# Linear attention on one core: the first head loaded whole, the last head's q work in halves, a longer warm-up matmul, and new per-engine orders

## Chip, core and metric

One core of a Trainium2 chip runs the whole program. The time is the device time of one execution in microseconds (us); lower is better. Eight executions of the kernel before are at hand, median 173.31 us, from 172.78 to 173.74.

## What is computed

Inputs q, k and v and the output have the shape (1, 32, 2048, 128) in bf16. For each of the 32 heads:

```python
phi(x) = where(x > 0, x + 1, exp(x)) + 1e-6
kv  = phi(k)^T @ v          # 128 x 128
z   = sum over s of phi(k)  # 128
out = (phi(q) @ kv) / (phi(q) . z + 1e-6)
```

## The kernel before, in words

A head's q, k and v are 2048 rows of 128. Partition p of the 128 holds rows 16p to 16p+15, so a whole head is one tile of 128 x (16 x 128), 4 KB a partition and 512 KB in all; half a head, 8 of the 16 rows, is 2 KB a partition. `phi` is split in two summands, min(exp(x), 1) + eps and max(x, 0), and each is multiplied by TensorE on its own, so they are never added up outside PSUM.

The steps of head h carry short keys, and these keys are what the orders are made of:

- `ldq`, `ldk`, `ldv` (L300, SP queue): the loads, into a ring of NI = 7 heads. `st` (L392, SP queue): the store, from a ring of NO = 12 heads. A load waits until the ring place is free, a store until its products are done. All go through one queue, in order.
- `ek` (L312, ACT): exp of k. `em` (L315, DVE): min with 1, plus eps. `rkd` (L318, DVE) and `rkp` (L322, POOL): max(k, 0) of rows 0 to 7 and of rows 8 to 15. `v1` (L326, POOL): a copy of v beside a column of ones.
- `kv` (L333, PE): 32 matmuls in two halves of 16 into one PSUM group. `kvs` (L338, ACT): its copy to SBUF.
- `T` (L344, PE): 16 transposes of q into PSUM. `eq` (L347, ACT): exp of it. `emq` (L349, DVE): min and eps. `rqa` (L353, ACT) and `rqb` (L356, DVE): max(q, 0) of rows 0 to 7 and 8 to 15. There is one transposed tile, so `T` of a head waits for `eq`, `rqa` and `rqb` of the head before.
- `n` (L363, L368, L370, PE): phi(q) times kv for 12 rows (`n.0`, four banks) and 4 rows (`n.1`, two banks), after a small matmul that sets eps. `r` (L377, DVE): reciprocal of the denominators. `f` (L384, DVE): the products, which also free the banks. The last head has three such groups of 6, 6 and 4 rows.
- `w` (L291, PE): matmuls of the identity into an unused bank, 120 columns each, in three groups of 60, 15 and 15 (`WARM`, L12). They compute nothing that is used; w2, and so the first of them in the order, waits for the identity.

What decides which rows a step covers are the functions `k_parts`, `q_parts`, `v_parts` (L17 to L21): two halves for head 0, whole for all others. In the kernel before, loads and steps share these.

The order of the work is written out by hand for each of the five engines (`ORDER`, L60 to L120) as a list of keys. `Program.resolve` (L158) works out the semaphore waits from the dependencies that `head` (L303) states; an engine executes its list strictly in order, so what stands behind a waiting step waits too. From head 3 on `gate` (L54) holds back the two POOL steps: `v1` of head h until `r.0` of head h - 3 is done, `rkp` until `f.0` of head h - 3 is done.

```python
def k_parts(h):
    return HALVES if h == 0 else WHOLE

q_parts = v_parts = k_parts
```

Of the kernel before, what the change touches and what calls it, by code (L numbers as in the profile page):

```python
# [21 lines left out]

# [31 lines left out]
def gate(name, h):  # L54
    if h < 3:
# [5 lines left out]
    "PE": """  # L61
        w2 T0.1 T0.0 w1 w0 T1.0 kv0.0 kv0.1 n0.0 kv1.0 kv1.1 T2.0 n0.1 n1.0 kv2.0 kv2.1 T3.0 n1.1 kv3.0 kv3.1 n2.0
        T4.0 n2.1 kv4.0 kv4.1 n3.0 T5.0 n3.1 kv5.0 kv5.1 n4.0 T6.0 n4.1 kv6.0 kv6.1 n5.0 T7.0 n5.1 kv7.0 kv7.1 n6.0
# [12 lines left out]
        f2.0 em5.0 rqb4 r2.1 rkd6.0 f2.1 r3.0 emq4.0 f3.0 em6.0 rqb5 r3.1 rkd7.0 f3.1 r4.0 emq5.0 f4.0 em7.0 rqb6
        r4.1 f4.1 r5.0 emq6.0 f5.0 em8.0 rqb7 r5.1 f5.1 rkd8.0 r6.0 emq7.0 f6.0 em9.0 rqb8 r6.1 f6.1 rkd10.0 rkd9.0
        r7.0 emq8.0 f7.0 rkd11.0 rqb9 r7.1 em10.0 f7.1 r8.0 emq9.0 f8.0 em11.0 rqb10 r8.1 f8.1 rkd12.0 r9.0 emq10.0
        f9.0 em12.0 r9.1 rqb11 f9.1 emq11.0 r10.0 rkd13.0 f10.0 em13.0 rqb12 r10.1 f10.1 rkd14.0 r11.0 emq12.0 f11.0
# [12 lines left out]
        eq0.1 eq0.0 rqa0 ek0.0 ek1.0 ek0.1 eq1.0 kvs0 rqa1 ek2.0 kvs1 ek3.0 eq2.0 rqa2 kvs2 ek4.0 eq3.0 kvs3 rqa3
        ek5.0 eq4.0 kvs4 rqa4 ek6.0 eq5.0 kvs5 rqa5 ek7.0 eq6.0 kvs6 rqa6 ek8.0 eq7.0 kvs7 rqa7 ek9.0 eq8.0 kvs8
# [14 lines left out]
    "SP": """  # L108
        ldq0.0 ldq0.1 ldk0.0 ldk0.1 ldk1.0 ldq1.0 ldv0.0 ldv0.1 ldv1.0 ldk2.0 ldq2.0 ldk3.0 ldv2.0 ldq3.0 ldk4.0
        ldv3.0 ldv4.0 ldq4.0 ldk5.0 ldv5.0 ldv6.0 ldq5.0 ldk6.0 ldk7.0 ldv7.0 ldk8.0 ldq6.0 ldk9.0 ldv8.0 ldq7.0  # L110
        ldq8.0 st0.0 ldk10.0 ldq9.0 st1.0 ldv9.0 ldv10.0 ldv11.0 ldq10.0 ldk11.0 ldk12.0 ldk13.0 ldv12.0 ldv13.0
        ldq11.0 st2.0 ldq12.0 st3.0 ldq13.0 ldq14.0 ldk14.0 ldv14.0 ldk15.0 ldv15.0 st4.0 ldk16.0 ldq15.0 ldk17.0
        ldq16.0 ldv16.0 ldv17.0 ldv18.0 ldk18.0 ldq17.0 ldk19.0 ldq18.0 st5.0 ldv19.0 ldk20.0 ldk21.0 ldq19.0
        ldq20.0 ldv20.0 ldv21.0 ldv22.0 ldv23.0 ldk22.0 st6.0 st7.0 st8.0 ldk23.0 ldq21.0 ldk24.0 ldq22.0 ldk25.0
        ldv24.0 ldk26.0 ldq23.0 ldq24.0 ldk27.0 st9.0 ldv25.0 st10.0 ldq25.0 ldv26.0 st11.0 ldq26.0 ldv27.0 st12.0
        ldk28.0 ldk29.0 ldq27.0 st13.0 ldv28.0 st14.0 ldk30.0 ldq28.0 ldv29.0 ldq29.0 ldq30.0 st15.0 ldv30.0 ldv31.0
        ldk31.0 ldq31.0 st16.0 st17.0 st18.0 st19.0 st20.0 st21.0 st22.0 st23.0 st24.0 st25.0 st26.0 st27.0 st28.0
        st29.0 st30.0 st31.0 st31.1 st31.2
    """,
# [97 lines left out]
def bass_standalone__linear_attn_elu__prompt_kernel(nc: bass.Bass, q: bass.AP, k: bass.AP, v: bass.AP, out: bass.AP):  # L217
# [11 lines left out]
    with ExitStack() as es:  # L229
# [73 lines left out]
        def head(h):  # L303
            for i, (a, b) in enumerate(k_parts(h)):
                load("k", k_sb, kf, h, i, a, b, freed(NI, h, ("ek", k_parts), ("rkd", rkd_parts), ("rkp", rkp_parts)))
            for i, (a, b) in enumerate(q_parts(h)):
                load("q", q_sb, qf, h, i, a, b, freed(NI, h, ("T", q_parts)))
            for i, (a, b) in enumerate(v_parts(h)):
                load("v", v_sb, vf, h, i, a, b, freed(NI, h, ("v1", v_parts)))

# [30 lines left out]
            for i, (a, b) in enumerate(q_parts(h)):  # L341
                def g(e, a=a, b=b):
                    for j in range(a, b):
                        ins = e.transpose(xT[:, j], q_sb[:, h % NI, j], ident[:])  # L344
# [2 lines left out]
                add("ACT", f"eq{h}.{i}", lambda e, a=a, b=b: e.activation(emq_sb[:, h % NQ, a:b], xT[:, a:b], ACT.Exp),  # L347
# [109 lines left out]
```

## Time and profile before

| what | value |
|---|---|
| median of 8 executions | 173.31 us (172.78 to 173.74) |
| profiled execution, its time | 173.48 us |
| its span, first to last instruction | 171.6 us |
| busy share: PE, PE weight load, DVE, ACT, POOL | 94%, 93%, 91%, 89%, 50% |
| granted TensorE clock, mean | 0.982 |
| data moved | 67.52 MB, 394 GB/s over the span |
| `eq` whole head, `ek` whole head (mean) | 1877 ns, 1912 ns, x31 each |
| `f` of 12 rows, `f` of 4 rows (mean) | 1744 ns, 682 ns |
| store at the end (128 KB), issue to landing | 1.8 us |

Durations are of one profiled execution. A row "18.21 0.28 ACT L338 ... [0.93 <-PE la L333]" means: at 18.21 us from the span's start ACT began line 338, which took 0.28 us, after 0.93 us without work which a step of PE's line 333 ended. Neighbouring durations overlap a little[...]; the distance between starts is what a step costs in a row of steps. Issues on the SP queue are not work: what counts for them is the landing, which is the time of the last of 16 completion events of a DMA.

### The profile page before, as it was taken

How to read it: one execution, taken by the hardware profiler on the slowest of the kernel's cores; microseconds unless marked ns; L12 is line 12 of the kernel's file. 1: busy time of each engine (PE TensorE's matmuls, PEld its weight loads, DVE VectorE, ACT ScalarE, POOL GpSimd, SP SyncE). 2: the span in 40 equal slices, each digit the busy share in tenths (PEclk: the TensorE clock that was granted, in tenths of full speed). 3: DMA queues.
4: the chain of work that ended last, by engine and by line, in shares of the span. 5: the costliest groups of instructions: out<-in, count | busy, mean ns of one | idle time of the engine just before them, and what ended most of it. 6: DMA issues, size and time to landing. Idle time of an engine off the chain costs nothing.

```text
span 171.6 us, 6462 instructions
## 1 busy us (share of the span) xinstructions
PE 161.3 (94%) x2842; PEld 158.9 (93%) x2842; DVE 156.2 (91%) x266; ACT 153.4 (89%) x131; POOL 85.2 (50%) x71
## 2 busy tenths in 40 slices
PE   3898989999999999999999999999999999999771
PEld 3898889999999999999999999999999999999770
DVE  0539999999999999999999999999999999999883
ACT  2699789999999999999999999999999999996600
POOL 1255545566644664556655566555555555463000
PEclk9999999999999999999999999999999999999975
DMA  4999999999999999999999999999999999999874
GB/s 163 359 421 407 408 408 410 408 404 420 410 415 407 412 417 410 416 410 406 416 412 411 411 415 416 407 411 416 415 415 419 413 425 410 416 415 415 324 305 146
DMA packets 19179, 67.52 MB, mean 394 GB/s; under 512 B 2128, under 2 KB 2512, under 8 KB 19152
## 3 DMA queue, kind: packets, MB, share of 16 engines
q1 hardware_dynamic: 19152, 67.12, 97.5%
q8 instruction: 22, 0.36, 0.8%
q14 instruction: 5, 0.04, 0.1%
HBM read 50.33 MB, written 16.78 MB: 391 GB/s over the span
## 4 chain that ended last, share of the span: by engine, by line
ACT 56%; PE 28%; DVE 11%; DMA 2%; issue 2%; SPq 0%; DVEq 0%
ACT la L347 22%; ACT la L312 21%; ACT la L353 10%; PE la L333 10%; PE la L368 6%; PE la L370 6%; PE la L344 5%; DVE la L384 5%; ACT la L338 3%; DMA la<-in_q_dram 2%; DVE la L318 2%; DVE la L349 2%; DVE la L315 1%; DVE la L356 1%; PE la L363 1%
## 5 line engine op out<-in xcount | busy, mean ns | idle before, releaser
L384 DVE TENSOR_TENSOR la<-la 128x1536 bf16<-128x1536 f32 (+2 forms) x65 | 77.7, 1197 | 0.7
L370 PE MATMUL la<-la 128*128 128x129 bf16 x512 | 69.1, 222 | 0.0
L368 PE MATMUL la<-la 128*128 128x129 bf16 x512 | 69.0, 220 | 0.0
L347 ACT ACTIVATE la<-la 128x2048 bf16<-128x2048 bf16 (+1 forms) x33 | 60.1, 1825 | 6.1 <-PE la L344 3.9
L333 PE MATMUL la<-la 128*128 128x129 bf16 x1024 | 64.0, 219 | 0.5 <-DVE la L315 0.5
L326 POOL COPY la<-la 128x1024 int32<-128x1024 int32 (+1 forms) x33 | 40.6, 1233 | 41.5 <-DVE la L377 34.2
L312 ACT ACTIVATE la<-la 128x2048 bf16<-128x2048 bf16 (+1 forms) x33 | 61.2, 1861 | 0.0
L333 PEld LDWEIGHTS la<-la 128*128 128x128 bf16 x1024 | 60.0, 97 | 0.7 <-DVE la L315 0.7
L322 POOL TENSOR_SCALAR la<-la 128x1024 bf16<-128x1024 bf16 x32 | 44.0, 1374 | 29.4 <-DVE la L384 23.8
L370 PEld LDWEIGHTS la<-la 128*128 128x128 bf16 x512 | 49.9, 97 | 0.0
L368 PEld LDWEIGHTS la<-la 128*128 128x128 bf16 x512 | 47.6, 98 | 0.0
L344 PE MATMUL la<-la 128*128 128x128 bf16 x512 | 34.6, 222 | 1.6 <-DMA la<-in_q_dram 1.6
L363 PE MATMUL la<-la 128*128 128x3 bf16 (+1 forms) x192 | 32.5, 169 | 2.9 <-DVE la L384 2.3
L353 ACT ACTIVATE la<-la 128x1024 bf16<-128x1024 bf16 x32 | 32.6, 1018 | 0.0
L344 PEld LDWEIGHTS la<-la 128*128 128x128 bf16 x512 | 30.0, 99 | 2.0 <-DMA la<-in_q_dram 1.8
L315 DVE TENSOR_SCALAR la<-la 128x2048 bf16<-128x2048 bf16 (+1 forms) x33 | 22.8, 695 | 2.9 <-ACT la L312 2.8
L349 DVE TENSOR_SCALAR la<-la 128x2048 bf16<-128x2048 bf16 (+1 forms) x33 | 22.6, 684 | 1.4 <-ACT la L347 1.3
L363 PEld LDWEIGHTS la<-la 128*128 128x128 bf16 x192 | 18.9, 98 | 4.4 <-DVE la L384 3.2
L356 DVE TENSOR_SCALAR la<-la 128x1024 bf16<-128x1024 bf16 x32 | 21.8, 680 | 1.2 <-ACT la L347 0.5
L318 DVE TENSOR_SCALAR la<-la 128x1024 bf16<-128x1024 bf16 x32 | 15.0, 475 | 5.5 <-DMA la<-in_k_dram 5.4
L377 DVE RECIPROCAL la<-la 128x12 f32<-128x12 f32 (+2 forms) x65 | 12.8, 198 | 1.1 <-PE la L370 0.4
L338 ACT ACTIVATE la<-la 128x129 bf16<-128x129 f32 x32 | 9.0, 282 | 1.5 <-PE la L333 1.5
(14 smaller groups left out, 15.9 us busy)
## 6 DMA issues: line engine op xcount, KB each, us to landing
la<-in_k_dram SPq DMA_DIRECT2D x31, 512.0 KB, 15.5
la<-in_q_dram SPq DMA_DIRECT2D x31, 512.0 KB, 15.5
la<-in_v_dram SPq DMA_DIRECT2D x31, 512.0 KB, 15.2
out_dram<-la SPq DMA_DIRECT2D x31, 512.0 KB, 15.2
la<-in_q_dram SPq DMA_DIRECT2D x2, 256.0 KB, 3.1
la<-in_k_dram SPq DMA_DIRECT2D x2, 256.0 KB, 4.1
la<-in_v_dram SPq DMA_DIRECT2D x2, 256.0 KB, 6.3
out_dram<-la SPq DMA_DIRECT2D x2, 192.0 KB, 2.1
```

The costliest lines, as they stand in the source:

```text
L312: add("ACT", f"ek{h}.{i}", lambda e, a=a, b=b: e.activation(em_sb[:, h % NE, a:b], k_sb[:, h % NI, a:b], ACT.Exp), [f"ldk{h}.{i}"] + freed ...
L322: add("POOL", f"rkp{h}.{i}", lambda e, a=a, b=b: e.tensor_scalar(rk_sb[:, h % NR, a:b], k_sb[:, h % NI, a:b], BIG, 0.0, op0=ALU.min, op1=A ...
L326: add("POOL", f"v1{h}.{i}", lambda e, a=a, b=b: e.tensor_copy(v1_sb[:, h % NV, a:b, 0:D].bitcast(i32), v_sb[:, h % NI, a:b].bitcast(i32)), ...
L333: ins = e.matmul(kv_ps, lhsT=src[:, j], rhs=v1_sb[:, h % NV, j, 0:NC], start=(j + part == 0), stop=(j == NT - 1 and part == 1))
L344: ins = e.transpose(xT[:, j], q_sb[:, h % NI, j], ident[:])
L347: add("ACT", f"eq{h}.{i}", lambda e, a=a, b=b: e.activation(emq_sb[:, h % NQ, a:b], xT[:, a:b], ACT.Exp), [f"T{h}.{i}"] + freed(NQ, h, ("n ...
L349: add("DVE", f"emq{h}.{i}", lambda e, a=a, b=b: e.tensor_scalar(emq_sb[:, h % NQ, a:b], emq_sb[:, h % NQ, a:b], 1.0, EPS, op0=ALU.min, op1 ...
L353: add("ACT", f"rqa{h}", lambda e: e.activation(rq_sb[:, h % NQ, 0:n], xT[:, 0:n], ACT.Relu), over("T", h, q_parts, 0, n) + freed(NQ, h, (" ...
L363: e.matmul(_ap(o_ps[:, :], o + D, [[NC, m]]), lhsT=ones[:], rhs=epsr[:, 0:m], start=True, stop=False, skip_group_check=True)
L368: e.matmul(to, lhsT=emq_sb[:, h % NQ, t], rhs=kvs_sb[:, h % NK], start=False, stop=False, skip_group_check=True)
L370: ins = e.matmul(to, lhsT=rq_sb[:, h % NQ, t], rhs=kvs_sb[:, h % NK], start=False, stop=True, skip_group_check=True)
L384: return e.tensor_tensor(out=_ap(o_sb[:, :, :, :], first(o_sb[:, h % NO, t0, 0:1]) - first(o_sb[:, :, :, :]), [[m * D, nb], [D, m], [1, D] ...
```

## The change

The loads of head 0 are whole, while its other steps stay in halves: a new `ld_parts` returns whole for every head, and each step that reads a load now waits for all loads that overlap its rows. `q_parts` gives halves for head 31 also, so that `T31`, `eq31` and `emq31` become two steps each. The warm-up matmul has 480 columns (the 120 columns of the identity read four times) and the groups are 15, 4 and 4. All five orders are new.

```diff
-WARM = (60, 15, 15)
+WARM = (15, 4, 4)
...
-q_parts = v_parts = k_parts
+def ld_parts(h):
+    return WHOLE
+
+
+v_parts = k_parts
+
+
+def q_parts(h):
+    return HALVES if h in (0, NH - 1) else WHOLE
...
     "PE": """
-        w2 T0.1 T0.0 w1 w0 T1.0 kv0.0 kv0.1 n0.0 kv1.0 kv1.1 T2.0 n0.1 n1.0 kv2.0 kv2.1 T3.0 n1.1 kv3.0 kv3.1 n2.0
+        w2 w1 T0.0 T0.1 w0 kv0.0 kv0.1 T1.0 n0.0 kv1.0 kv1.1 T2.0 n0.1 n1.0 kv2.0 kv2.1 T3.0 n1.1 kv3.0 kv3.1 n2.0
...
-        kv28.1 n27.0 T29.0 n27.1 kv29.0 kv29.1 n28.0 T30.0 n28.1 kv30.0 kv30.1 n29.0 T31.0 n29.1 kv31.0 kv31.1 n30.0
-        n30.1 n31.0 n31.1 n31.2
+        kv28.1 n27.0 T29.0 n27.1 kv29.0 kv29.1 n28.0 T30.0 n28.1 kv30.0 kv30.1 n29.0 T31.0 n29.1 T31.1 kv31.0 kv31.1
+        n30.0 n30.1 n31.0 n31.1 n31.2
...
     "DVE": """
-        rkd0.0 ones v1ones0 emq0.1 rqb0 emq0.0 rkd1.0 em0.0 em0.1 v1ones1 eps0 eps1 em1.0 eps2 emq1.0 rqb1 r0.0 f0.0
-        rkd3.0 rkd2.0 em2.0 em3.0 rqb2 emq2.0 r0.1 f0.1 r1.0 rkd4.0 f1.0 em4.0 rqb3 r1.1 rkd5.0 f1.1 r2.0 emq3.0
+        rkd0.0 v1ones0 v1ones1 eps0 ones em0.0 eps1 rkd1.0 em0.1 rqb0 eps2 emq0.0 emq0.1 em1.0 r0.0 f0.0 rqb1 rkd2.0
+        emq1.0 rkd3.0 em2.0 r1.0 em3.0 rqb2 emq2.0 r0.1 f0.1 f1.0 rkd4.0 em4.0 rkd5.0 r1.1 rqb3 f1.1 r2.0 emq3.0
...
-        rqb29 r27.1 emq29.0 f27.1 r28.0 em30.0 f28.0 em31.0 rqb30 r28.1 f28.1 r29.0 rkd31.0 f29.0 emq30.0 emq31.0
-        rqb31 r29.1 r30.0 f29.1 f30.0 r30.1 f30.1 r31.0 f31.0 r31.1 f31.1 r31.2 f31.2
+        rqb29 r27.1 rkd30.0 f27.1 r28.0 emq29.0 f28.0 em31.0 rqb30 r28.1 f28.1 r29.0 rkd31.0 f29.0 emq30.0 rqb31
+        r29.1 emq31.0 f29.1 r30.0 f30.0 r30.1 emq31.1 f30.1 r31.0 f31.0 r31.1 f31.1 r31.2 f31.2
...
     "ACT": """
-        eq0.1 eq0.0 rqa0 ek0.0 ek1.0 ek0.1 eq1.0 kvs0 rqa1 ek2.0 kvs1 ek3.0 eq2.0 rqa2 kvs2 ek4.0 eq3.0 kvs3 rqa3
+        rqa0 eq0.1 ek0.0 ek0.1 eq0.0 ek1.0 kvs0 eq1.0 rqa1 ek2.0 kvs1 ek3.0 eq2.0 rqa2 kvs2 ek4.0 eq3.0 kvs3 rqa3
...
-        ek30.0 eq29.0 kvs29 rqa29 ek31.0 eq30.0 kvs30 rqa30 eq31.0 rqa31 kvs31
+        ek30.0 eq29.0 kvs29 rqa29 ek31.0 eq30.0 kvs30 rqa30 eq31.1 eq31.0 kvs31 rqa31
...
     "SP": """
-        ldq0.0 ldq0.1 ldk0.0 ldk0.1 ldk1.0 ldq1.0 ldv0.0 ldv0.1 ldv1.0 ldk2.0 ldq2.0 ldk3.0 ldv2.0 ldq3.0 ldk4.0
+        ldq0.0 ldk0.0 ldv0.0 ldk1.0 ldq1.0 ldv1.0 ldk2.0 ldq2.0 ldk3.0 ldv2.0 ldk4.0 ldq3.0 ldv3.0 ldk5.0 ldq4.0
...
-                ins = e.matmul(o_ps[:, 512 + 3 * NC:512 + 3 * NC + 120], lhsT=ident[:], rhs=ident[:, 0:120],
+                ins = e.matmul(o_ps[:, 512:992], lhsT=ident[:], rhs=_ap(ident[:, :], 0, [[0, 4], [1, 120]]),
...
-            for i, (a, b) in enumerate(q_parts(h)):
+            for i, (a, b) in enumerate(ld_parts(h)):
                 load("q", q_sb, qf, h, i, a, b, freed(NI, h, ("T", q_parts)))
...
-                    [f"ldk{h}.{i}"] + freed(NE, h, ("kv", kv_parts)))
+                    over("ldk", h, ld_parts, a, b) + freed(NE, h, ("kv", kv_parts)))
```

On POOL one pair is exchanged (`v13.0` now ahead of `rkp3.0`). In the SP list the loads of the last heads stand later: `ldv31` is the 113th transfer in units of 512 KB instead of the 110th, `ldq31` the 116th instead of the 112th. In the middle DVE's list is made of the same steps per head, in a few rotations of `emq`, `r`, `rkd` and `rqb`.

More of the change, by code (lines that the diff above doesn't have):

```diff
@@ L75 @@
-        rkd3.0 rkd2.0 em2.0 em3.0 rqb2 emq2.0 r0.1 f0.1 r1.0 rkd4.0 f1.0 em4.0 rqb3 r1.1 rkd5.0 f1.1 r2.0 emq3.0
[L76 to L79, printed above, removed]
@@ L80 @@
-        em14.0 r11.1 rqb13 f11.1 rkd15.0 r12.0 emq13.0 f12.0 em15.0 r12.1 rqb14 f12.1 rkd16.0 r13.0 emq14.0 f13.0
-        em16.0 r13.1 rqb15 f13.1 rkd17.0 r14.0 emq15.0 f14.0 em17.0 r14.1 rqb16 f14.1 rkd18.0 r15.0 emq16.0 f15.0
-        em18.0 rqb17 r15.1 rkd19.0 f15.1 r16.0 emq17.0 f16.0 em19.0 rqb18 r16.1 rkd20.0 f16.1 r17.0 emq18.0 f17.0
-        em20.0 rqb19 r17.1 rkd21.0 f17.1 r18.0 emq19.0 f18.0 em21.0 rqb20 r18.1 f18.1 rkd22.0 r19.0 emq20.0 f19.0
-        em22.0 rqb21 r19.1 f19.1 rkd23.0 r20.0 emq21.0 f20.0 em23.0 rqb22 r20.1 rkd24.0 f20.1 r21.0 emq22.0 f21.0
@@ L85 @@
-        em24.0 r21.1 rqb23 f21.1 emq23.0 r22.0 rkd25.0 f22.0 em25.0 rqb24 r22.1 f22.1 rkd26.0 emq24.0 r23.0 f23.0
-        em26.0 r23.1 rqb25 f23.1 emq25.0 r24.0 rkd27.0 f24.0 em27.0 rqb26 r24.1 f24.1 emq26.0 r25.0 f25.0 em28.0
-        rqb27 r25.1 f25.1 rkd29.0 r26.0 rkd28.0 f26.0 emq27.0 rqb28 em29.0 r26.1 f26.1 r27.0 rkd30.0 f27.0 emq28.0
-        rqb29 r27.1 emq29.0 f27.1 r28.0 em30.0 f28.0 em31.0 rqb30 r28.1 f28.1 r29.0 rkd31.0 f29.0 emq30.0 emq31.0
-        rqb31 r29.1 r30.0 f29.1 f30.0 r30.1 f30.1 r31.0 f31.0 r31.1 f31.1 r31.2 f31.2
+        rkd0.0 v1ones0 v1ones1 eps0 ones em0.0 eps1 rkd1.0 em0.1 rqb0 eps2 emq0.0 emq0.1 em1.0 r0.0 f0.0 rqb1 rkd2.0
@@ new lines @@
+        emq1.0 rkd3.0 em2.0 r1.0 em3.0 rqb2 emq2.0 r0.1 f0.1 f1.0 rkd4.0 em4.0 rkd5.0 r1.1 rqb3 f1.1 r2.0 emq3.0
+        f2.0 em5.0 r2.1 rqb4 f2.1 rkd6.0 r3.0 emq4.0 f3.0 em6.0 rqb5 r3.1 f3.1 emq5.0 r4.0 rkd7.0 f4.0 em7.0 r4.1
+        rqb6 f4.1 emq6.0 r5.0 rkd8.0 f5.0 em8.0 rqb7 r5.1 rkd9.0 f5.1 r6.0 emq7.0 f6.0 em9.0 r6.1 rqb8 f6.1 rkd10.0
+        r7.0 emq8.0 f7.0 em10.0 rqb9 r7.1 f7.1 rkd11.0 r8.0 emq9.0 f8.0 em11.0 r8.1 rqb10 f8.1 emq10.0 r9.0 rkd12.0
+        f9.0 em12.0 r9.1 rqb11 f9.1 rkd13.0 r10.0 emq11.0 f10.0 em13.0 r10.1 rqb12 f10.1 emq12.0 r11.0 rkd14.0 f11.0
@@ new lines @@
+        em14.0 rqb13 r11.1 rkd15.0 f11.1 r12.0 emq13.0 f12.0 em15.0 rqb14 r12.1 f12.1 rkd16.0 r13.0 emq14.0 f13.0
+        em16.0 r13.1 rqb15 f13.1 emq15.0 r14.0 rkd17.0 f14.0 em17.0 rqb16 r14.1 f14.1 emq16.0 r15.0 rkd18.0 f15.0
+        em18.0 rqb17 r15.1 rkd19.0 f15.1 r16.0 emq17.0 f16.0 em19.0 rqb18 r16.1 rkd20.0 f16.1 r17.0 emq18.0 f17.0
+        em20.0 rqb19 r17.1 rkd21.0 f17.1 r18.0 emq19.0 f18.0 em21.0 r18.1 rqb20 f18.1 emq20.0 r19.0 rkd22.0 f19.0
+        em22.0 rqb21 r19.1 rkd23.0 f19.1 r20.0 emq21.0 f20.0 em23.0 r20.1 rqb22 rkd24.0 f20.1 r21.0 emq22.0 f21.0
@@ new lines @@
+        em24.0 rqb23 r21.1 f21.1 rkd25.0 r22.0 emq23.0 f22.0 em25.0 rqb24 r22.1 rkd26.0 f22.1 r23.0 emq24.0 f23.0
+        em26.0 r23.1 rqb25 f23.1 emq25.0 r24.0 rkd27.0 f24.0 em27.0 r24.1 rqb26 f24.1 r25.0 emq26.0 f25.0 em28.0
+        rqb27 rkd28.0 r25.1 f25.1 r26.0 emq27.0 f26.0 em29.0 rqb28 r26.1 rkd29.0 f26.1 r27.0 emq28.0 f27.0 em30.0
+        rqb29 r27.1 rkd30.0 f27.1 r28.0 emq29.0 f28.0 em31.0 rqb30 r28.1 f28.1 r29.0 rkd31.0 f29.0 emq30.0 rqb31
+        r29.1 emq31.0 f29.1 r30.0 f30.0 r30.1 emq31.1 f30.1 r31.0 f31.0 r31.1 f31.1 r31.2 f31.2
@@ L97 @@
         ek22.0 eq21.0 kvs21 rqa21 ek23.0 eq22.0 kvs22 rqa22 ek24.0 eq23.0 kvs23 rqa23 ek25.0 eq24.0 kvs24 rqa24
-        ek26.0 eq25.0 kvs25 rqa25 ek27.0 eq26.0 kvs26 rqa26 ek28.0 eq27.0 kvs27 rqa27 ek29.0 eq28.0 rqa28 kvs28
-        ek30.0 eq29.0 kvs29 rqa29 ek31.0 eq30.0 kvs30 rqa30 eq31.0 rqa31 kvs31
+        ek26.0 eq25.0 kvs25 rqa25 ek27.0 eq26.0 kvs26 rqa26 ek28.0 eq27.0 kvs27 rqa27 ek29.0 eq28.0 kvs28 rqa28
+        ek30.0 eq29.0 kvs29 rqa29 ek31.0 eq30.0 kvs30 rqa30 eq31.1 eq31.0 kvs31 rqa31
     """,
     "POOL": """
-        ident0 ident rkp0.0 v10.0 v10.1 v11.0 rkp1.0 rkp2.0 v12.0 rkp3.0 v13.0 v14.0 rkp4.0 v15.0 rkp5.0 v16.0
+        ident0 ident rkp0.0 v10.0 v10.1 v11.0 rkp1.0 rkp2.0 v12.0 v13.0 rkp3.0 v14.0 rkp4.0 v15.0 rkp5.0 v16.0
         rkp6.0 v17.0 rkp7.0 v18.0 rkp8.0 v19.0 rkp9.0 v110.0 rkp10.0 v111.0 rkp11.0 v112.0 rkp12.0 v113.0 rkp13.0
@@ L108 @@
     "SP": """
-        ldq0.0 ldq0.1 ldk0.0 ldk0.1 ldk1.0 ldq1.0 ldv0.0 ldv0.1 ldv1.0 ldk2.0 ldq2.0 ldk3.0 ldv2.0 ldq3.0 ldk4.0
[L110 to L118, printed above, removed]
+        ldq0.0 ldk0.0 ldv0.0 ldk1.0 ldq1.0 ldv1.0 ldk2.0 ldq2.0 ldk3.0 ldv2.0 ldk4.0 ldq3.0 ldv3.0 ldk5.0 ldq4.0
+        ldv4.0 ldk6.0 ldv5.0 ldq5.0 ldq6.0 ldv6.0 ldv7.0 ldq7.0 ldk7.0 ldk8.0 ldv8.0 ldk9.0 ldv9.0 st0.0 ldv10.0
+        ldq8.0 ldk10.0 ldq9.0 ldk11.0 ldk12.0 ldq10.0 ldv11.0 ldv12.0 ldq11.0 st1.0 st2.0 ldk13.0 ldv13.0 ldq12.0
+        ldk14.0 ldq13.0 ldv14.0 ldk15.0 ldq14.0 ldq15.0 ldv15.0 ldv16.0 ldq16.0 ldv17.0 ldq17.0 ldk16.0 ldk17.0
+        ldv18.0 ldk18.0 st3.0 ldq18.0 ldq19.0 ldk19.0 st4.0 ldk20.0 ldk21.0 ldq20.0 ldv19.0 ldk22.0 ldq21.0 ldq22.0
+        st5.0 ldv20.0 st6.0 ldv21.0 ldq23.0 ldk23.0 st7.0 ldq24.0 ldv22.0 ldk24.0 ldk25.0 ldv23.0 st8.0 st9.0
+        ldv24.0 ldv25.0 st10.0 ldq25.0 ldq26.0 ldk26.0 st11.0 st12.0 ldv26.0 ldk27.0 ldv27.0 ldk28.0 ldk29.0 ldq27.0
+        ldv28.0 ldv29.0 st13.0 ldk30.0 ldq28.0 st14.0 ldv30.0 ldq29.0 st15.0 ldk31.0 st16.0 st17.0 ldq30.0 ldv31.0
+        st18.0 st19.0 ldq31.0 st20.0 st21.0 st22.0 st23.0 st24.0 st25.0 st26.0 st27.0 st28.0 st29.0 st30.0 st31.0
+        st31.1 st31.2
     """,
@@ L303, in head @@
         def head(h):
-            for i, (a, b) in enumerate(k_parts(h)):
+            for i, (a, b) in enumerate(ld_parts(h)):
                 load("k", k_sb, kf, h, i, a, b, freed(NI, h, ("ek", k_parts), ("rkd", rkd_parts), ("rkp", rkp_parts)))
-            for i, (a, b) in enumerate(q_parts(h)):
+            for i, (a, b) in enumerate(ld_parts(h)):
                 load("q", q_sb, qf, h, i, a, b, freed(NI, h, ("T", q_parts)))
-            for i, (a, b) in enumerate(v_parts(h)):
+            for i, (a, b) in enumerate(ld_parts(h)):
                 load("v", v_sb, vf, h, i, a, b, freed(NI, h, ("v1", v_parts)))
@@ L319, in head @@
                     rk_sb[:, h % NR, a:b], k_sb[:, h % NI, a:b], 0.0, None, op0=ALU.max),
-                    over("ldk", h, k_parts, a, b) + freed(NR, h, ("kv", kv_parts)))
+                    over("ldk", h, ld_parts, a, b) + freed(NR, h, ("kv", kv_parts)))
             for i, (a, b) in enumerate(rkp_parts(h)):
@@ L323, in head @@
                     rk_sb[:, h % NR, a:b], k_sb[:, h % NI, a:b], BIG, 0.0, op0=ALU.min, op1=ALU.max),
-                    over("ldk", h, k_parts, a, b) + freed(NR, h, ("kv", kv_parts)) + gate("rkp", h))
+                    over("ldk", h, ld_parts, a, b) + freed(NR, h, ("kv", kv_parts)) + gate("rkp", h))
             for i, (a, b) in enumerate(v_parts(h)):
@@ L327, in head @@
                     v1_sb[:, h % NV, a:b, 0:D].bitcast(i32), v_sb[:, h % NI, a:b].bitcast(i32)),
-                    [f"ldv{h}.{i}"] + freed(NV, h, ("kv", kv_parts)) + gate("v1", h))
+                    over("ldv", h, ld_parts, a, b) + freed(NV, h, ("kv", kv_parts)) + gate("v1", h))
             for i, (a, b) in enumerate(kv_parts(h)):
@@ L345, in g @@
                     return ins
-                add("PE", f"T{h}.{i}", g, [f"ldq{h}.{i}", "ident"] + ((every("eq", h - 1, q_parts) + rqs(h - 1)) if h else []))
+                add("PE", f"T{h}.{i}", g, over("ldq", h, ld_parts, a, b) + ["ident"] + ((every("eq", h - 1, q_parts) + rqs(h - 1)) if h else []))
                 add("ACT", f"eq{h}.{i}", lambda e, a=a, b=b: e.activation(emq_sb[:, h % NQ, a:b], xT[:, a:b], ACT.Exp),
```

## The prediction

> **What bounds the kernel now.** I read the page first for the engines, then the DMA share by stretches of time, then ACT's and DVE's timelines at both ends.
>
> ```profile
> PE 161.3 (94%) x2842; PEld 158.9 (93%) x2842; DVE 156.2 (91%) x266; ACT 153.4 (89%) x131; POOL 85.2 (50%) x71
> ...
> ACT 56%; PE 28%; DVE 11%; DMA 2%; issue 2%; SPq 0%; DVEq 0%
> ```
>
> Four resources are nearly full, and the chain is mostly ACT. From one `ek` to the next it is 4.725 us in nearly all heads between 28 and 147 us: `ek` 1.80, `eq` 1.77, `rqa` 0.91, `kvs` 0.24. No order shortens that sum. So the time is when ACT gets going, 32 heads at 4.725, ACT's few gaps, and what follows ACT's last step.
>
> ```profile
> 3.00:4.50 1.50, 0.23 (x3) 0.00 (x0) 0.00 (x0) 0.00 (x0) 0.00 (x0) 1.00 0.71 234
> 4.50:6.50 2.00, 1.70 (x17) 1.70 (x18) 0.61 (x3) 0.63 (x1) 0.00 (x0) 1.00 1.02 332
> ...
> 15.00:158.00 143.00, 141.92 (x2567) 140.53 (x2565) 140.51 (x237) 140.02 (x119) 79.35 (x60) 1.00 1.03 413
> ...
> 162.00:164.00 2.00, 0.75 (x12) 0.50 (x10) 1.99 (x5) 0.00 (x0) 0.00 (x0) 1.00 0.63 248
> ```
>
> The last two columns are DMA share and GB/s. The DMA queue is full from 4.5 to 158 us, at 413 GB/s or 1.27 us per 512 KB. It is a second bound just behind the first: 128 such transfers are 162.6 us. Only the first 4.5 us and the last 10 have air.
>
> ```profile
> 18.21 0.28 ACT L338 ACTIVATE la<-la 128x129 bf16<-128x129 f32 x1 [0.93 <-PE la L333]
> ...
> 23.57 0.28 ACT L338 ACTIVATE la<-la 128x129 bf16<-128x129 f32 x1 [0.60 <-PE la L333]
> ...
> 158.81 1.88 ACT L347 ACTIVATE la<-la 128x2048 bf16<-128x2048 bf16 x1 [1.70 <-PE la L370]
> ...
> 161.49 0.28 ACT L338 ACTIVATE la<-la 128x129 bf16<-128x129 f32 x1
> ...
> 162.26 2.29 DVE L384 TENSOR_TENSOR la<-la 128x512 bf16<-128x512 f32 x2
> ...
> 168.27 0.69 DVE L384 TENSOR_TENSOR la<-la 128x512 bf16<-128x512 f32 x1
> ```
>
> ACT starts `eq0` at 5.87 and loses 0.93 + 0.60 us in the opening, both times on `kv`. At the end it waits 1.70 for `n29`, and is done at 161.8. Then DVE works off `f29` to `f31` until 168.96; the last store lands at 170.83 by the trace, 0.8 before the span ends.
>
> **Whole loads of head 0.** Three DMAs fewer; each issue takes 0.43 us on SP. By landing events the halves of q landed at 3.29 and 4.75, those of k at 5.42 and 6.54, `k1` at 7.80, those of v at 9.77 and 10.43. The first five transfers, halves, thus follow each other at 1.1 to 1.4 us, as long as a whole one takes later. Here a rule speaks against the change: the Trainium skill, "DMA: Bandwidth & Descriptors", section "Specifications", puts line rate at 512 B and more per piece, so 2 KB pieces lose nothing and whole loads win nothing. The trace is against it for the opening (234 GB/s from 3.0 to 4.5 us), but for it at 8.0 to 9.5 us, where halves of v moved at 399 GB/s behind a full queue. So the loss is one of starting, not of piece size alone. By the rule the stream gains 0; by the row, 1.418 MB moved up to 6.5 us, where 0.38 MB/us from 1.9 on (the 4 KB rate at 6 to 7 us) would give 1.75, a gain of 0.33 / 0.41 = 0.8 us; from the landings (`q0` about 4.0, then 1.27 each: `k0` 5.3, `v0` 6.5, `k1` 7.8, against positions 3 and 7 at 7.80 and 12.99 before, now 6.5 and 11.6) 1.3. I take 1.0, with 0 and 1.3 as ends.
>
> **Warm-up.** Before, 120 columns took 0.101 us start to start until 8.3 us, then 0.053. 480 columns are then 0.40 us cold and 0.20 (the 0.053 times four, 0.21 at most) warm. w2 and w1, 8 of them, fill 1.53 to 4.75, so `T0.0` starts at 4.75, as before (4.80), although q is there earlier: the earlier landing of q is worth nothing by itself. w0, 15 of them, lies ahead of `kv0`. If the clock rises at 8.31 as before, `T0` ends at 6.46, and w0 at 8.31 + (15 - 4.6) x 0.203 = 10.4. The skill's "TensorE: Matmul & The Clock Gate", section "Part 1: The HAM clock gate", says that the array is released after about one busy window of 3.4 us, in windows that run free of the kernel. The trace fits: 3.5 us of work without a pause from 4.80 to 8.3. With no pause from 1.53 on the rise would lie between 4.9 and 8.35 by that rule, and w0 would end between 8.8 and 10.4. I use both ends.
>
> **The opening, walked.** Durations are starts to starts: a half exp 0.95, a whole one 1.80. ACT: `rqa0` 5.8 (5.5 with an early clock), `eq0.1`, `ek0.0`, `ek0.1`, `eq0.0`, `ek1` until 12.4 (12.1). `em0.1` is done at about 10.0, v's copies (POOL, 0.67 each, after `v0` at 6.5) at 8.0. Before, `ek0.1` ended only at 12.45, as `ek1` stood ahead of it; that wait of DVE (2.3 us) goes.
> - Late clock: `kv0` 10.4 to 12.3, `kvs0` 12.5, `T1`, which now stands behind it, until 13.2, so `eq1` at 13.4 after 0.7 us of idle ACT; `ek2` 16.1, `kvs1` 17.9 without a wait (`n0.0` to 14.6, `kv1` to 16.4), `ek4` at 22.85. Before: 23.75. Gain 0.9.
> - Early clock: `kv0` 9.0 to 10.9, `T1` to 11.95, no idle; `n0.0` 12.6 to 14.0, `kv1` to 15.9, `ek4` at 21.8; with one slowed DVE step (below) `kv2` ends 0.4 later and `ek4` is at 22.2. Gain 1.5 to 1.95.
> I take 1.2; the ends are 0.3 and 1.95. What is late next is `T3` and `kv3`, PE being as full as ACT (1.84 + 0.91 + 1.9 = 4.65 a head). Waits of `ek` and `v1` for loads: `v2`, 18.32 before, at about 17.2, its copy 18.3, needed by `kv2` at 19.5; `v4`, two places later in the queue, at 24.9 and needed by `kv4` at about 28.5. No wait.
>
> **The new orders in the middle.** 27 heads at 4.725. DVE was busy 83.99 of 85.00 us from 60 to 145, so 1.0 us of play. The rotations now used are mostly among those of before, which all ran at 4.725: `rkd` between `r.0` and `f.0` (heads 10, 22, 24 before) took 0.36 us with POOL's copy starting 0.15 behind it. One irregular head before cost ACT 0.35 us (`ek11` to `ek12`: 5.08), two late ones 0.1 and 0.3. I take a gain of 0.2, ends -1.0 and +0.4. Loads: by place in the queue each lands at least 1.5 us ahead of need in the middle (smallest `v20`, 99.4 against 101); `v31` 150.9 against 153.2, `q31` 154.5 against 157.7, before counting the earlier stream. Stores 12 heads back land at least 1.9 ahead of the `f` that reuses their place. Nothing.
>
> **The end.** PE: `T31` in two, 0.46 each, with `n29.1` between: same sum; `eq31.1` starts about 158.9 (as `eq31` before, 158.81). Two halves are 0.95 each, 0.13 more than one, but `rqb31` needs only the first: 159.9, so DVE's idle 0.47 before `emq31` goes, `emq31.1` moves behind `f30.0`, and `f29.1` starts at 161.35 instead of 162.26. `f30.0` then ends at 164.0 instead of 164.5, `n31` follows it, and DVE's gaps of 0.24 and 0.17 close, as `emq31.1` and `f30.1` (1.1 us) cover `n31.0`. DVE ends at 168.3: 0.65. I take 0.6; ends 0.2 and 0.8.
>
> **Sum.** Compute: 1.2 + 0.2 + 0.6 = 2.0. The queue: its FIFO ran full up to `st28` (165.93) and `st29` (167.25, 1.3 later); `st30` and `st31` behind it without a pause would land at 168.5 and 169.8. With the stream 1.0 earlier that is 168.8, against 170.83: gain at most 2.0. Two limits at the same place seldom meet without loss, so I take 1.8: 173.48 - 1.8 = 171.7 for the profiled run (span 169.8), and 171.5 from the median, which lies 0.17 below.
>
> **Rivals.**
> - *The stream does not gain* (the rule holds). Then the last store cannot land before 169.8: gain 1.0, 172.3. For: 2 KB pieces at 399 GB/s at 8 us. Against: 234 GB/s at 3 us. Chance 0.15.
> - *w0 in the way*: a clock that rises about two us later than 8.3 (10.4) has w0 end at 10.4 + (15 - 9.9) x 0.203 = 11.4 and `kv0` at 13.3; ACT then idles 1.1 ahead of `kvs0` and 0.7 ahead of `eq1`, 1.8 against 1.53 before: opening -0.2, total 0.6: 172.8. Chance 0.10.
> - *Slower: DVE meets POOL in the middle.* Place: `rkd` and `emq` around `r.0`, which release POOL's copy. Price: `rkd2` and `rkd3` took 1.25 each beside POOL at 18.4 to 20.9, `rkd` else 0.36 to 0.42, so 0.8 each. It decides when DVE's play (1.0) and the gain (1.8) are used up, at 3.5 such meetings. Six: +2.0, 175.3; four to five, 174.2, the likeliest form. Against: those rotations ran clean before. Chance 0.12.
> - *The orders only trade places*, opening won, DVE and PE give it back through the ring of waits: 173.3. Chance 0.05.
> - Forecast as summed, 170.8 to 172.2: 0.58.
>
> About 0.2% (0.35 us) is what a measurement can tell from no change. Faster: 0.58 + 0.15 + 0.06 of the second rival; same: 0.04 + 0.05; slower: 0.12. Range 170.8 to 173.4: all but the slower rival and the tip of the forecast, 0.84.
>
> **What would show it.** ACT's `ek4` at 22 to 23 instead of 23.75, no 0.93 gap at `kvs1`; 512 KB landings at 4, 5.3, 6.5 us and DMA near 380 GB/s before 4.5 us; `ek` to `ek` 4.725 in the middle; DVE without gaps after 159 and its last step near 166.9; `st29` to `st31` landing in close order. Wrong if `w0` ends after 12 us, if `rkd` or `emq` means rise above 0.5 and 0.7, or if the last stores come one by one with a pause, which would leave the end to compute alone.

## The result, and the profile after

The changed kernel takes 171.86 us (median of 11 executions, 171.21 to 172.32) against 173.28 for the kernel before (32 executions on the same chip): a ratio of 0.9921, 95% interval 0.9906 to 0.9935, so 1.4 us less. The profiled execution took 171.56, its span is 169.8. The prediction of 171.5 was 0.4 us too low. That its size came out nearly right is in part luck: of its two terms compute gained more than was forecast, and the DMA queue less. Here and below a median is over all executions, and a ratio leaves out the four that were over 1.5% above the fastest of their kernel.

The page after, engines and chain:

```profile
PE 159.0 (94%) x2775; PEld 153.4 (90%) x2775; DVE 153.1 (90%) x267; ACT 153.0 (90%) x132; POOL 85.0 (50%) x71
...
ACT 73%; PE 17%; DVE 6%; issue 1%; POOL 0%; POOLq 0%
```

ACT and DVE do the same work in a shorter span, PE the same but for 67 fewer warm-up matmuls, and the chain is ACT's for 73% of it instead of 56%. On its timeline (start, duration, engine and line, idle before it) the opening and the end read:

```profile
5.25 1.02 ACT L361 ACTIVATE la<-la 128x1024 bf16<-128x1024 bf16 x1 [3.23 <-PE la L352]
...
11.68 0.29 ACT L346 ACTIVATE la<-la 128x129 bf16<-128x129 f32 x1
11.92 1.88 ACT L355 ACTIVATE la<-la 128x2048 bf16<-128x2048 bf16 x1
...
21.36 0.28 ACT L346 ACTIVATE la<-la 128x129 bf16<-128x129 f32 x1 [0.20 <-PE la L341]
21.54 1.90 ACT L320 ACTIVATE la<-la 128x2048 bf16<-128x2048 bf16 x1
...
156.08 1.94 ACT L355 ACTIVATE la<-la 128x1024 bf16<-128x1024 bf16 x2 [1.77 <-PE la L352]
```

`ek4`, at 23.75 before, starts at 21.54; of the gaps of 0.93 and 0.60 us only 0.20 is left. DVE's last product (the row of 164.82) ends at 165.51, where it ended at 168.96:

```profile
159.65 1.76 DVE L392 TENSOR_TENSOR la<-la 128x1536 bf16<-128x1536 f32 x1
...
164.82 0.69 DVE L392 TENSOR_TENSOR la<-la 128x512 bf16<-128x512 f32 x1
```

So compute ends 3.45 us earlier, and the span is only 1.8 shorter. The difference stands in the DMA views. First the stretches of time (last two columns: DMA share and GB/s), then the issues of stores with their KB and the us from issue to landing:

```profile
3.00:4.50 1.50, 1.50 (x5) 0.60 (x4) 0.00 (x0) 0.00 (x0) 0.00 (x0) 1.00 1.02 404
4.50:6.50 2.00, 2.00 (x23) 1.38 (x21) 0.66 (x5) 1.25 (x2) 1.14 (x1) 1.00 1.00 324
...
164.00:166.00 2.00, 0.00 (x0) 0.00 (x0) 1.48 (x3) 0.00 (x0) 0.00 (x0) 1.00 0.86 326
166.00:168.00 2.00, 0.00 (x0) 0.00 (x0) 0.00 (x0) 0.00 (x0) 0.00 (x0) 1.00 0.67 247
```

```profile
out_dram<-la SPq DMA_DIRECT2D x2, 192.0 KB, 3.1
out_dram<-la SPq DMA_DIRECT2D x1, 128.0 KB, 3.5
```

From 166 us on no engine works, and the queue still moves 247 GB/s. The last store (128 KB) took 1.84 us from issue to landing before; now it is issued at 165.54 and lands at 169.04, 3.5 us later, behind what is left. The stream is 170 GB/s faster than before from 3.0 to 4.5 us (404 against 234), but not from 4.5 to 6.5 (324 against 332), and the store of head 28 lands at 165.22, only 0.7 earlier than before.

### The profile page after: what moved, and what is told of

Same layout as the page of the kernel before. It is cut to its first block, busy times and chain, and to the rows that moved or that the text cites. A ratio compares the mean times of both kernels' runs of the same rounds, so it can differ in the third digit from the quotient of the medians.

```text
span 169.8 us, 6325 instructions
## 1 busy us (share of the span) xinstructions
PE 159.0 (94%) x2775; PEld 153.4 (90%) x2775; DVE 153.1 (90%) x267; ACT 153.0 (90%) x132; POOL 85.0 (50%) x71
## 4 chain that ended last, share of the span: by engine, by line
ACT 73%; PE 17%; DVE 6%; issue 1%; POOL 0%; POOLq 0%
ACT la L320 29%; ACT la L355 27%; ACT la L361 13%; PE la L341 5%; DVE la L392 4%; ACT la L346 4%; PE la L376 4%; PE la L378 3%; PE la L352 3%; PE la L299 2%; DVE la L364 1%; DVE la L385 1%; DVE la L326 0%; PE la L371 0%; DVE la L357 0%
## 5 line engine op out<-in xcount | busy, mean ns | idle before, releaser
L352 PE MATMUL la<-la 128*128 128x128 bf16 x512 | 33.9, 219 | 0.9 <-DVE la L364 0.9
L323 DVE TENSOR_SCALAR la<-la 128x2048 bf16<-128x2048 bf16 (+1 forms) x33 | 22.8, 689 | 2.7 <-ACT la L320 2.7
L364 DVE TENSOR_SCALAR la<-la 128x1024 bf16<-128x1024 bf16 x32 | 21.5, 673 | 0.0
L357 DVE TENSOR_SCALAR la<-la 128x2048 bf16<-128x2048 bf16 (+1 forms) x34 | 21.5, 633 | 0.0
L326 DVE TENSOR_SCALAR la<-la 128x1024 bf16<-128x1024 bf16 x32 | 14.5, 452 | 5.7 <-DMA la<-in_k_dram 5.6
L385 DVE RECIPROCAL la<-la 128x12 f32<-128x12 f32 (+2 forms) x65 | 12.9, 198 | 3.2 <-PE la L378 1.8
```

The costliest lines, as they stand in the source:

```text
L364: add("DVE", f"rqb{h}", lambda e: e.tensor_scalar(rq_sb[:, h % NQ, n:], xT[:, n:], 0.0, None, op0=ALU.max), over("eq", h, q_parts, n, NT) ...
```

## Experiments

Theory Q: two limits stand at the end, DVE's last product plus 1.9 us for its store, and the DMA queue's backlog; before the first was later, now the second. Rival C: compute alone sets the end. All times below are medians, each beside the kernel before on the same chip (173.18 to 173.23). Times within a span are of one profiled execution; landings are read from the completion events of its trace.

### Four stores less

```diff
-            for i, (a, b) in enumerate(st_parts(h)):
+            for i, (a, b) in enumerate(st_parts(h) if h >= 4 else ()):
```

> The kernel before, with the stores of heads 0 to 3 left out (not written). Theory Q: before, the last product (168.96 us) and not the queue set the end, the last store landed 1.84 us after its issue; so no change beyond 0.3 us: 173.0 to 173.4. A rival in which the queue limits both kernels alike: 1 us or more less, 172.3 or below.

The kernel before, less four stores: 173.15 against 173.18, ratio 1.0004 (0.9980 to 1.0028). Its queue was not the limit, as Q says.

> The changed kernel, with the stores of heads 0 to 3 left out (2 MB less through the queue; those four heads of the output are not written). Theory Q, the end of the changed kernel is set by the full DMA queue: the last product is done at 165.5 us and only the backlog keeps the last store until 169.04; without 4 x 1.27 us of transfers the last store lands about 1.9 us after the last product, at 167.4, so about 1.5 us less: 170.2 to 170.5. Rival C, the end is set by the compute alone: within 0.3 us of 171.9.

The changed kernel, less four stores: 172.56 (170.76 to 173.75). Only one execution of twelve, 170.76, came near Q's 170.2 to 170.5; taken by its median this spoke against Q and for neither theory, as it was slower than the changed kernel itself. Its profiled execution, the slowest of the twelve, had ACT waiting 2.2 us ahead of `eq3` and `eq4`, with DVE's `emq2` at 1.55 us instead of 0.68, and `rkd4` and `em4` at 1.20 and 1.52 instead of 0.42 and 0.69; each ran beside a POOL step. Here `emq2` follows POOL's copy, and in the changed kernel's trace it runs ahead of it:

```profile
21.72 1.04 POOL L333 COPY la<-la 128x1024 int32<-128x1024 int32 x1 [4.26 <-DVE la L322]
21.76 1.55 DVE L356 TENSOR_SCALAR la<-la 128x2048 bf16<-128x2048 bf16 x1
...
20.89 0.68 DVE L357 TENSOR_SCALAR la<-la 128x2048 bf16<-128x2048 bf16 x1
21.50 1.04 POOL L334 COPY la<-la 128x1024 int32<-128x1024 int32 x1 [2.34 <-DVE la L364]
```

That gave theory P: in the new opening DVE can meet POOL's steps for heads 3 and 4. The traces also show when: with the TensorE clock. In the eight traces of the new opening with the long warm-up matmul the clock rose at 4.2, 4.5, 5.3, 5.7, 6.1, 6.5, 6.9 and 7.2 us, and one of `emq2`, `rkd4` and `em4` takes over 1 us in the last three only. A late clock makes `T0` slow; first the changed kernel, then this run:

```profile
4.61 1.06 PE L352 MATMUL la<-la 128*128 128x128 bf16 x16
...
4.70 1.91 PE L351 MATMUL la<-la 128*128 128x128 bf16 x16
```

With it `w0` ends later and stands in the way of `kv0`, which begins at 9.87 us here and at 8.80 there. The run with hardly any warm-up, further down, has its clock at 12.9 us and the meeting too. That a late clock brings the meeting is read from these nine executions, not from a run made for it.

### The changed kernel again, and one wait more

> The changed kernel once more, unaltered, beside the next three on one chip. In the trace of the changed kernel with four stores less, DVE's emq of head 2 began 40 ns after POOL's copy of v for head 3 and took 1.55 us instead of 0.68, and rkd4 and em4 then met POOL's next two steps (1.20 and 1.52 instead of 0.42 and 0.69). Theory P: whether this happens depends on when the clock rises and v3 lands, so here the time is 171.7 to 172.7, and the profile has either emq2 at 0.7 (ek6 near 31.0) or at 1.5 (ek6 near 34). Rival: the meeting came from the missing stores; then 171.9 and emq2 at 0.7.

171.82 (171.70 to 172.20), six executions. The profile, of the slowest of them, has `emq2`, `rkd4` and `em4` at 0.68, 0.42 and 0.69, so no meeting there (`rkd3` met POOL's copy for head 2 and took 1.26); the last product ends at 165.82, the last store landed at 169.68.

```profile
165.13 0.69 DVE L392 TENSOR_TENSOR la<-la 128x512 bf16<-128x512 f32 x1
```

```diff
+    if (name, h) == ("v1", 3):
+        return ["r0.1"]
     return [f"r{h - 3}.0"] if name == "v1" else [f"f{h - 3}.0"]
```

> The changed kernel with one more wait: POOL's copy of v for head 3 waits for r.1 of head 0 (it waited for r.0 of head 0), so that it falls beside f0.1 and f1.0 and not beside emq2. Theory P: emq2 0.7 in every run, so the slow cases go: 0 to 0.8 us below the changed kernel of the same chip, highest run nearer the median. Rival: the meeting is rare or hidden by the queue: same within 0.2 us.

172.10 (171.82 to 172.20): no gain from the wait. In the profiled execution `emq2` was 0.68 as wanted, but `rkd4` (25.10) and `em4` (26.09) met POOL's copy for head 4 (24.85) and the step behind it:

```profile
25.10 1.07 DVE L328 TENSOR_SCALAR la<-la 128x1024 bf16<-128x1024 bf16 x1
26.09 1.52 DVE L325 TENSOR_SCALAR la<-la 128x2048 bf16<-128x2048 bf16 x1
27.53 0.41 DVE L328 TENSOR_SCALAR la<-la 128x1024 bf16<-128x1024 bf16 x1
```

ACT then waits 1.2 us on `n2`, and the last product ends at 167.28:

```profile
166.59 0.69 DVE L394 TENSOR_TENSOR la<-la 128x512 bf16<-128x512 f32 x1
```

Whether the wait or the late clock (6.5 us) moved the meeting is open: the next kernel, with the same wait and a rise at 6.1, had none.

This misfired repair speaks for Q. Beside the trace of the unaltered kernel its compute ends 1.46 us later (167.28 against 165.82), and its last store lands 0.48 earlier (169.20 against 169.68), because in that execution the backlog drained earlier (store of head 28 at 164.78 against 165.91). The two traces are of the slowest execution of the one and the fastest of the other, so the 0.48 is no difference of kernels; in the medians the loss of 1.46 in compute shows as at most 0.28.

> The same with the stores of heads 0 to 3 left out (not written). Theory Q, the backlog of the queue hides 1.6 us of what compute gained: 170.0 to 170.7, 1.3 us or more below the kernel with that wait and all stores, and the last store lands about 1.9 us after its issue. Rival C, compute alone sets the end: no difference to it.

171.68, only 0.4 below the kernel with all stores: the expectation fails by its median. But the ten executions fell into two groups: five from 170.60 to 171.09 and five from 172.26 to 172.99. The profiled one (171.0) has the last product at 166.18 and its store landed at 168.05, 1.85 after its issue; in the stretch from 162 to 164 us the queue has run dry:

```profile
162.00:164.00 2.00, 1.87 (x36) 1.88 (x37) 1.96 (x6) 0.00 (x0) 0.00 (x0) 1.00 0.14 49
```

So without a backlog the span ends with compute, and 171.0 is 0.8 us below the changed kernel although its last product is 0.4 later than there: Q. The second group is not profiled; that it is executions with the meeting of DVE and POOL is argued from the size (1.8 us, where ACT waited 1.2 and 2.2 in the two profiled cases), not shown.

The times of the two kernels with four stores less also hold 0.3 us that are not the span's: time less span is 2.15 and 2.19 us on average, and 1.86 in the changed kernel. By spans the lower group has 168.4 to 168.9 and the kernel with the wait and all stores 169.9 to 170.4, so the gain is 1.4, as Q forecast; the upper group has 170.1 to 170.8, at or a little above the spans with all stores, so that most such executions would not stand out there. Not settled is the changed kernel less four stores: its median span of 170.4 is the highest with all stores (169.3 to 170.4), as if the meeting were more frequent in it, and how often the meeting occurs in either was not counted.

### Loads of head 0 alone

```diff
 def ld_parts(h):
-    return WHOLE
+    return HALVES if h == 0 else WHOLE
```

> The changed kernel with only head 0's loads back in halves (three more DMAs, 2 KB pieces; everything else as changed). Theory Q: the stream of transfers loses the 0.7 us by which the store of head 28 landed earlier, and the end with it: 172.3 to 172.7. The rule that 2 KB pieces move at line rate, with the opening the only source of the gain: no change, 171.7 to 172.0.

172.76 (ratio to before 0.9976, 0.9953 to 1.0000), a little above the range of Q: going back to halves costs 0.9 us of the 1.4. The store of head 28 landed at 166.49, 0.6 to 1.3 later than in the two executions with whole loads, and the last store at 170.24, 3.8 us after its issue; compute ended at 166.37. The low rate of the opening is back, 228 GB/s as against 404 and 401 in the two executions with whole loads:

```profile
3.00:4.50 1.50, 1.50 (x6) 0.58 (x5) 0.00 (x0) 0.00 (x0) 0.00 (x0) 1.00 0.87 228
```

Whether the size of the pieces or the three more transfers make it was not separated.

> The kernel before with only head 0's loads whole (its orders otherwise unchanged). Theory Q: the stream is about 0.7 us earlier, but the end is DVE's, and ACT starts by q as before (the whole q lands at 4.0 instead of 4.75, so at most 0.7 earlier, and em, v1 wait as before): 172.7 to 173.3. Rival, whole loads are the main gain: 172.3 or below.

172.74, ratio 0.9977 (0.9956 to 0.9998): whole loads alone, with the old orders, give 0.4 us, as Q allowed. No trace of a usual execution is at hand, so by which path the 0.4 comes was not seen.

### The opening alone

> The kernel before with head 0 loaded whole and the changed order of PE, DVE, ACT and POOL for the opening only (up to the step em2 on DVE, ek3 on ACT, kv3 on PE); the rest of the orders, the end and the old warm-up matmul (120 columns, the same number of columns in all) as before. Theory Q: the opening gains about 2 us of compute, the stream 0.7, so the end comes to 169.0 in the span or a little later: 171.9 to 172.3, nearly the whole gain. Rival, the gain needs the new end: 172.5 or above.

173.65 (172.27 to 175.88), ratio 1.0014 (0.9982 to 1.0045), no gain: the expectation fails. The profile says why. In the old order of SP `v0` is the fifth transfer, and POOL waited for it until 10.35:

```profile
10.35 2.54 POOL L330 COPY la<-la 128x512 int32<-128x512 int32 x3 [3.72 <-DMA la<-in_v_dram]
```

`kvs0` came at 13.14, `T1` stands behind `kv0` in the new order, `eq1` began at 14.03, later than before (12.45), and `ek4` at 23.28, so of 2 us in the opening 0.5 is left. The orders of the engines need the order of the loads.

```diff
     "SP": """
-        ldq0.0 ldk0.0 ldk1.0 ldq1.0 ldv0.0 ldv1.0 ldk2.0 ldq2.0 ldk3.0 ldv2.0 ldq3.0 ldk4.0
+        ldq0.0 ldk0.0 ldv0.0 ldk1.0 ldq1.0 ldv1.0 ldk2.0 ldq2.0 ldk3.0 ldv2.0 ldk4.0 ldq3.0
```

> The kernel before with head 0 loaded whole, the changed opening of PE, DVE, ACT and POOL, and now the changed order of SP as well, so that v0 is the third transfer and not the fifth; middle and end of the engines' lists and the warm-up matmul as before. If v0's late landing (10.3 us, kvs0 at 13.1) was what spoilt the run without SP's order: kvs0 near 11.7, ek4 21.5 to 22.1, 171.8 to 172.4. If the old middle cannot use the opening: 172.8 or above.

172.26, ratio 0.9952 (0.9931 to 0.9973), inside the first range. `kvs0` at 12.06 and `ek4` at 22.05:

```profile
12.06 0.29 ACT L342 ACTIVATE la<-la 128x129 bf16<-128x129 f32 x1
12.80 1.88 ACT L351 ACTIVATE la<-la 128x2048 bf16<-128x2048 bf16 x1 [0.44 <-PE la L348]
...
22.05 1.95 ACT L316 ACTIVATE la<-la 128x2048 bf16<-128x2048 bf16 x1
```

The clock rose at 7.1 us here, and ACT waited 0.44 for `T1`. The opening with its loads gives 0.97 of the 1.4 us, with the old middle, the old end and the old warm-up matmul.

### The end alone

```diff
-    return HALVES if h in (0, NH - 1) else WHOLE
+    return HALVES if h == 0 else WHOLE
```

> The changed kernel with head 31's q steps whole again and the end of the old lists (PE from n29.1, ACT from rqa30, DVE from f29.0 on). Theory Q: the last product comes about 0.6 us later, at 166.1 to 166.5, and the last store lands when the queue is empty all the same: no change, 171.7 to 172.1. Rival C, compute sets the end: 0.6 us more, 172.4 or above.

172.31 (171.27 to 173.45), 0.5 us above the changed kernel: between Q and C, so Q's "no change" was too strong. The profiled execution (173.45, its slowest) shows both things at once: the meeting, with `emq2`, `rkd4` and `em4` long,

```profile
21.60 1.22 DVE L357 TENSOR_SCALAR la<-la 128x2048 bf16<-128x2048 bf16 x1
...
25.22 1.17 DVE L326 TENSOR_SCALAR la<-la 128x1024 bf16<-128x1024 bf16 x1
26.31 1.52 DVE L323 TENSOR_SCALAR la<-la 128x2048 bf16<-128x2048 bf16 x1
```

while POOL runs its steps for head 3 and head 4,

```profile
21.24 1.04 POOL L334 COPY la<-la 128x1024 int32<-128x1024 int32 x1 [2.47 <-DVE la L323]
22.24 1.47 POOL L330 TENSOR_SCALAR la<-la 128x1024 bf16<-128x1024 bf16 x1
25.07 1.04 POOL L334 COPY la<-la 128x1024 int32<-128x1024 int32 x1 [1.35 <-issue]
```

and the old end, 10.73 us from `eq31` to the last product, against 9.43 after and 10.15 before. Its product ends at 168.91 and the store lands at 170.81. Either delay by itself seems to stay below the backlog, as the extra wait showed for the meeting (167.28) and the lowest execution here (171.27) suggests for the old end; both together do not. So the new end would be worth little in a clean execution and pay when the opening goes badly; that is argued from these few executions.

### The warm-up

```diff
-WARM = (15, 4, 4)
+WARM = (1, 1, 1)
```

> The changed kernel with one warm-up matmul in each group instead of 15, 4 and 4. PE is then idle from about 6 to 8.8 us, and kv0, T1 and n0 run at half the clock: kv0 1.8 us longer, T1 0.9, so eq1 starts about 2 us later (near 14 instead of 11.9) and ek4 2 to 3 us later. Theory Q: up to 1.6 us of that is hidden by the queue, so 172.2 to 173.6. Rival C: all of it shows, 173.9 or above. Rival, the warm-up is not needed (the transposes keep the clock up): 172.0.

172.41, ratio to before 0.9958 (0.9938 to 0.9978): 0.6 us above the changed kernel, in Q's range, far from C's, and 0.4 above that of a warm-up without use. The granted clock is at half until 12.9 us, `kv0` runs at 0.108 us a matmul, `eq1` begins at 13.64 (11.92 or 12.27 with warm-up) and `ek4` at 22.89:

```profile
12.42 0.28 ACT L346 ACTIVATE la<-la 128x129 bf16<-128x129 f32 x1 [0.74 <-PE la L341]
13.64 1.88 ACT L355 ACTIVATE la<-la 128x2048 bf16<-128x2048 bf16 x1 [0.93 <-PE la L352]
```

With two steps of DVE (`emq2` 1.49, `em4` 1.53) meeting POOL besides, the last product is at 168.03, 2.2 later than in the unaltered kernel, of which 0.6 us appears.

### The last stores on another queue

```diff
-                add("SP", f"st{h}.{i}", ...
+                add("ACT" if h >= 29 else "SP", f"st{h}.{i}", ...
```

> The changed kernel with the stores of heads 29 to 31 issued by ACT, which is done by then, so on another queue. If the backlog is one of the 16 DMA engines, which both queues share, st31 passes the backlog but st26 to st28 land later by as much: the same end, 171.6 to 172.1. If it belongs to the SP queue alone, the last store lands 1.9 us after its issue and the end is the compute's: 170.4 to 170.8.

172.07, no gain, as expected for a backlog that sits in the shared DMA engines: the store of head 28 landed at 167.09 instead of 165.2 to 165.9, and the last one at 169.57, 3.1 us after its issue.

## Point by point

**Opening: right, and larger.** Forecast 1.2 (0.3 to 1.95), measured 2.2 at `ek4`, and 1.8 in the second execution. The walk for an early clock (`eq1` at 12.1, `ek4` at 21.8) is what happened: 11.92 and 21.54, then 12.27 and 21.94. The clock rose at 4.5 us, with the eight matmuls done at 4.61 and `T0` at the full rate, and at 5.3 in the second execution, in the middle of `T0`. That it was early in these two is luck: the prediction had it between 4.9 and 8.35, and the traces have it from 4.2 to 7.2. The chance given to a `w0` in the way was not needed here, as `w0` ended at 8.5 and `kv0` began at 8.8; with the clock at 6.1 us and later `kv0` began as soon as `w0` ended, at 9.3 to 9.9. ACT began at 5.25.

**Middle: right.** 0.5 (0.2 forecast): `ek` to `ek` 4.725 in nearly all heads, two irregular ones of 0.06 and 0.29.

**End: right.** 0.72 (0.6 forecast): from `eq31` to the last product 9.43 us instead of 10.15. DVE has no gap above 0.15 us after 157 us.

**Sum of compute: too small.** 2.0 forecast, 3.45 and 3.14 in two executions; the sum took the low side of the opening.

**The stream: too large, and this term set the time.** 1.0 forecast (ends 0 and 1.3). By the store of head 28 it is 0.7 in one execution and 0.0 in the other; the difference in time from going back to halves is 0.9. The failing step is the line of landings after `q0`: `q0` at 4.04 (forecast 4.0) and `k0` at 5.28 (5.3) fit, then `v0` came at 7.80 instead of 6.5 and `k1` at 9.06 instead of 7.8. By the prediction's own measure the stream gained next to nothing: the third and the seventh 512 KB landed at 7.80 and 12.99 before, and at 7.80 and 12.87 after. A landing is the last of 16 completions, and these had drifted apart: the first of `v0` was there at 6.27, fourteen by 7.08, two at 7.8. The first completion of the seventh came 0.6 earlier than before (11.59 against 12.18), and so did that of the store of head 28 (160.01 against 160.62). The rate of 324 GB/s from 4.5 to 6.5 us, at a DMA share of 1.00, is the same as before the change (332), so what slows the queue there is neither the size of the loads nor the change; its cause was not found. A slip stands in the forecast's reading too: the halves before landed 1.46, 0.67 and 1.12 us apart, not 1.1 to 1.4, and the fifth transfer, `k1`, was whole.

The queue as the limit to compute's gain was right, and so was its sum: without a pause the last store lands at 169.8 less what the stream gains. With gains of 0.7 and 0.0 that is 169.1 and 169.8, and 169.04 and 169.68 were measured. The second execution, at 172.20, is thus the first rival, a stream that does not gain (172.3).

**The rule on piece size.** Loads in halves do lose here: 0.9 us in the changed kernel, 0.4 in the one before, measured. The rule that the prediction set against the change does not cover the first microseconds of this queue, and there the row (234 GB/s) was the better guide, although not in its amount.

**The slower rival was real, in another place.** DVE meets POOL, at 0.5 to 0.9 us a meeting as priced (0.8), but between 21 and 28 us, where `v13`, `rkp3`, `v14` and `rkp4` follow the landings of `v3` and `v4`, and not at `r.0` in the middle. The opening moved up by 2 us and these landings by under 1, which brings them close to `emq2` and `em4`; with a late clock `emq2` falls behind the copy. That it does not make the kernel slower fits Q, in which the backlog covers one such chain. The forecast saw neither the place nor that cover. The Trainium skill, "SBUF — State Buffer", section "SBUF: two separate sides", would give the size: DVE, in a mode that uses two ports or with two inputs in SBUF, and GpSimd share one port pair, and whichever starts first holds it for its whole instruction. That `emq2` runs in such a mode no run here shows; the times fit. In the trace with four stores less `emq2` began at 21.76, 40 ns after the copy, and ended at 23.31, 0.55 after the copy's end at 22.76, where it takes 0.68 alone; starting ahead of the copy in the changed kernel (20.89 against 21.50) it took 0.68.

## What to carry to other kernels

When a transfer queue is busy for nearly the whole span, write down two ends, compute's last step plus its store, and the queue's last byte; a change is worth what the later of the two moves by, and the gap between them says how much delay is free. To speed up the opening of such a kernel, move the loads together with the steps that read them: here the orders without the loads' order gave nothing. A wait that repairs one collision may leave the next pair to collide, as in the one trace here, so look at the whole chain of steps on both engines before adding it. And look at the start of several executions: here one profile alone would have shown the early clock and no meeting.

## What was not expected of the hardware

The 16 completions of one transfer drift apart over the run: the store of head 28 has its first at 160.01 and its last at 165.22, and `q1`, early on, 9.03 and 10.32. The end of the queue is the end of its latest part; issuing the last stores on another queue did not get round it (3.1 us from issue to landing). The trace points to a cause. Beside the kernel's transfers the same DMA engines carry instructions:

```profile
q8 instruction: 22, 0.36, 0.8%
```

These are 22 packets of 16 KB, each of about 1 us. Just after the first, at 15.56 us, one completion of `v2` falls behind (17.70, the next to last 16.70), and in the kernel before, after the first at 13.14, one of `q2` (15.77 against 14.26). From 15 to 155 us the lags of the 16 completions behind the first of them grow from 6 to 44 us in sum, while 26 instruction packets, these and some of 8 KB, take 23 us. That they cause the drift is argued from this; no run changes them.

The TensorE clock rose at very different times in executions that start alike. In the eight traces with the 480-column warm-up and PE busy without a pause from 1.53 us on, it rose 2.7 to 5.7 us later (4.2 to 7.2); with 120-column matmuls and the new opening at 7.1 and 7.5, in the kernel before at 8.3. So the rise at 4.5 us in the changed kernel's profile is one draw from a spread; that the longer matmul brings it forward is not shown, only that a warm-up of one matmul a group delays it (12.9).
